# Draining a PSUM pair with two engines, one bank each, in a fused attention and maxout-FFN kernel

## The chip, the cores and the metric

The kernel runs on one core of one Trainium2 chip. The time is the device time of that core in microseconds; lower is better.

## The reference

Attention over 32 memory slots, for 8 batches of 8 heads, 576 positions and 64 dimensions, and behind it a feed-forward layer that takes the maximum of three products:

```python
def _attn_ref(q, k, v, phi):
    a = np.exp(phi - np.max(phi, axis=2, keepdims=True))
    a = a / (np.sum(a, axis=2, keepdims=True) + 1e-09)      # over the positions
    k_m = np.einsum('bhsm,bhsd->bhmd', a, k)
    v_m = np.einsum('bhsm,bhsd->bhmd', a, v)
    scores = (1.0 / np.sqrt(q.shape[-1])) * np.matmul(q, k_m.transpose(0, 1, 3, 2))
    attn = np.exp(scores - np.max(scores, axis=-1, keepdims=True))
    attn = attn / (np.sum(attn, axis=-1, keepdims=True) + 1e-09)
    return np.matmul(attn, v_m)
def _moe_ref(x, w1, w2, w3, w_out):
    h = np.maximum(np.maximum(x @ w1, x @ w2), x @ w3)
    return h @ w_out
```

`x` is the attention's output with the heads side by side: 4608 rows of 512 columns. `w1`, `w2`, `w3` are 512 x 768 and `w_out` is 768 x 512.

## The kernel before

The kernel never forms `x`. It multiplies the 32 value vectors of each head with the weights first (a *fold*), so that the feed-forward layer works on the attention weights: 256 numbers per position in place of 512. And it writes max(x w1, x w2, x w3) as x w3 + max(x (w1 - w3), x (w2 - w3), 0), so that only two products need a maximum and the third goes with `w_out` straight to the output.

Every step is a *piece*, named by a letter, a number and the batch, and the list of pieces at the end of the kernel is the order in which they are issued. Each engine runs its own instructions in this order and waits by semaphores for what it needs. There is no other scheduler. The pieces are:

- L, r: loads of phi, k, v and q on GpSimd's queue (`load_ph`, `load_kv`, `load_q`), and copies of k and v to a packed tile on GpSimd (`pack`). E: exponential of phi, on ScalarE.
- B, N, K: matmuls of phi's exponentials with k, v and ones (`att_kv`), the division on VectorE, and a transpose through TensorE with a small copy (`att_kv_t`, tile kvt).
- Q, S: transposes of q on VectorE, and the scores with their two exponentials on ScalarE (`att_score`, line 347). a, s, c, m, X: the softmax, that is a transpose, a sum and a reciprocal on VectorE, a product on GpSimd (line 414) and a transpose back into `attn` on VectorE (line 422), each for two groups of heads.
- D: folds (`fold`, line 445). D0 to D2 fold `w1 - w3` and `w2 - w3` in 512 columns each, D3 folds `w3 w_out`. A fold writes two banks of PSUM, one per group of heads.
- F: the first layer (`ffn1`, line 471), 12 pieces per batch of four matmuls with 288 columns, in two banks, one per half of the positions. Six are drained with relu into `h1`, and six by VectorE, which takes the maximum of the piece and `h1` (line 484).
- P, T: the second layer (`ffn2`, lines 502, 532, 541): 36 output tiles of 128 rows in one bank each, six matmuls with the hidden tile `hT` and two with `attn`. P starts a tile with three of them. T drains it and stores it from SyncE's queue.

PSUM has eight banks, and the digits behind `banks` give each piece its bank, or the first of two, in the order of the pieces. A piece whose bank is still being drained makes TensorE wait. The table `EVAC` says which engine drains which kind of piece, and `!` behind a piece swaps the two:

```python
EVAC = {"D": "avaaa", "T": "vavav", "K": "v", "W": "vvv", "O": "aaaa", "F": "aaaaaa"}
def evacuate(kind, n, swap, out_, in_, relu=False):
    if (EVAC[kind][n] == "a") != swap:
        ...   # ScalarE: activation with Relu, or copy
    ...       # VectorE: tensor_scalar_max, or tensor_copy
```

Of the kernel before, what the change touches and what calls it, by code (L numbers as in the profile page):

```python
# [15 lines left out]
def kernel(  # L16
# [12 lines left out]
    nc = tc.nc  # L29

    B, H, S, D = q.shape
    M = phi.shape[-1]
    P = 128
    NP = H // 2
    NG = NP // 2
    HP = P // 2
# [4 lines left out]
    FT = DF // P  # L41
    SH = S // 2
    BANK = 512
    HEAD = 3
# [96 lines left out]
    for i in range(P // M):  # L141
# [4 lines left out]
    banks = iter(  # L146
        "".join(
            """
            60606026024506010445024062406246024602434403424206026420462406240723043240604602
            46026402645260502624620640264024601642102461462624604624260462045260024062404206  # L150
            12640264014206502402605220462406420462036040432402677670
            """.split()
        )
    )
# [1 line left out]
    def one_bank():  # L156
        return psum[:, int(next(banks))]
# [13 lines left out]

    EVAC = {"D": "avaaa", "T": "vavav", "K": "v", "W": "vvv", "O": "aaaa", "F": "aaaaaa"}

    def evacuate(kind, n, swap, out_, in_, relu=False):

        if (EVAC[kind][n] == "a") != swap:
            if relu:
                nc.scalar.activation(out=out_, in_=in_, func=AF.Relu)  # L178
            else:
                nc.scalar.copy(out=out_, in_=in_)  # L180
        elif relu:
            nc.vector.tensor_scalar_max(out=out_, in0=in_, scalar1=0.0)  # L182
        else:
            nc.vector.tensor_copy(out=out_, in_=in_)  # L184

    def w3_t(f2, swap):
# [7 lines left out]
                )  # L194
        evacuate("W", f2, swap, w3T[:, 2 * f2 : 2 * f2 + 2], pt)

    def w3_o(j, swap):
        po = one_bank()
        for f in range(FT):
            nc.tensor.matmul(  # L200
                po,
                lhsT=w3T[:, f, j, :],
                rhs=wo_sb[:, f, :],
                start=(f == 0),
                stop=(f == FT - 1),
            )
        evacuate("O", j, swap, w3o[:, j, :], po)
# [115 lines left out]
    attns = {}  # L323
# [168 lines left out]

    heads = {}

    def ffn2_head(b, t):

        hT = hts[b // 2]
        c0 = (b % 2) * (S + HP) + t * P
        po = heads[b, t] = one_bank()
        for n in range(HEAD):  # L500
            fc = fts[b][n]
            nc.tensor.matmul(  # L502
                po,
                lhsT=hT[:, fc, c0 : c0 + P],
                rhs=wo_sb[:, fc, :],
                start=(n == 0),
                stop=False,
            )

    def ffn2(b, t, swap):  # L510


        hT, attn = hts[b // 2], attns[b // 2]
        c0 = S - HP if t == 4 else (b % 2) * (S + HP) + t * P
        if b == B - 1 and t == 3:
            return ffn2_last(b, c0)
        po = heads[b, t] if (b, t) in heads else one_bank()

        if t == 4:
            for g in range(NG):  # L520
                for u in range(2):
                    nc.tensor.matmul(  # L522
                        po[HP * u : HP * (u + 1)],
                        lhsT=attn[:, g, c0 + HP * u : c0 + HP * (u + 1)],
                        rhs=wp3s[b - 1 + u][:, g, :],
                        start=(g == 0),
                        stop=False,
                        tile_position=(0, HP * u),
                    )
        for n in range(HEAD if (b, t) in heads else 0, FT):  # L530
            fc = fts[b][n]
            nc.tensor.matmul(  # L532
                po,
                lhsT=hT[:, fc, c0 : c0 + P],
                rhs=wo_sb[:, fc, :],
                start=(n == 0 and t < 4),
                stop=(n == FT - 1 and t == 4),
            )
        if t < 4:
            for g in range(NG):  # L540
                nc.tensor.matmul(  # L541
                    po,
                    lhsT=attn[:, g, c0 : c0 + P],
                    rhs=wp3s[b][:, g, :],
                    start=False,
                    stop=(g == NG - 1),
                )
        ot = opool.tile([P, DM], FP32, name="ot")
        r0 = (b // 2) * 2 * S + c0
        rows = out[r0 : r0 + P, :]  # L550
        evacuate("T", t, swap, ot, po)
        nc.sync.dma_start(out=rows, in_=ot)
# [33 lines left out]
    def issue(b, n, swap):  # L586

        i = int(n[1:]) if len(n) > 1 else None
        {
            "I": lambda: [make_identity(nc, ident)]  # L590
            + [nc.gpsimd.memset(x[:, :, :, 2 * D : 2 * D + 1], 1.0) for x in kvrs],
            "Y": lambda: load_w(i) if i < 3 else load_wo(),
            "L": lambda: load_ph(b) if i == 0 else load_q(b) if i == 3 else load_kv(b, i - 1),
            "H": lambda: load_kv(b, i % 2, halves[i // 2]),
            "r": lambda: pack(b, i),
            "E": lambda: [att_exp(b, h) for h in (halves if b == 0 else [slice(0, NP)])],
            "B": lambda: att_kv(b, i),
            "N": lambda: att_kv_norm(b, i),
            "K": lambda: att_kv_t(b, swap, i),
            "Q": lambda: att_q(b, i),  # L600
            "S": lambda: att_score(b),
            "a": lambda: att_t(b, i),
            "s": lambda: att_sum(b, i),
            "c": lambda: att_rec(b, i),
            "m": lambda: att_mul(b, i),
            "X": lambda: (ones_mul if (b, i) in ONES else att_back)(b, i),
            "M": lambda: ones_sum(b, i),
            "R": lambda: ones_rec(b, i),
            "D": lambda: fold(b, i, swap),
            "F": lambda: ffn1(b, i, swap),  # L610
            "P": lambda: ffn2_head(b, i),
            "T": lambda: ffn2(b, i, swap),
            "W": lambda: w3_t(i, swap),
            "O": lambda: w3_o(i, swap),
            "V": lambda: w_diff(i),
            "G": lambda: wait_for(b, i),
            "Z": lambda: warm_up(i),
        }[n[0]]()


    for w in """
        E@0 H0@0 H2@0 L3@0 Z25@0 B0@0 I@0 N0@0 Z2@0 K0@0! Q0@0 Q1@0 Z9@0 S@0 Z2@0 M0@0 M1@0
        R0@0 Y2@0 G0@0 R1@0 W0@0 Y3@0 W1@0 W2@0 Z6@0 O1@0 H3@0 O3@0 O2@0 H1@0 X1@0 B1@0 X0@0
        N1@0 K1@0 O0@0 Y0@0 D1@0! D0@0! D3@0 F8@0 F10@0 F2@0 V0@0 F6@0 F0@0! Y1@0 D2@0 L0@1
        V2@0 L1@1 D4@0 V1@0 L3@1 F4@0 F3@0 L2@1 L1@2 F1@0 L2@2 F7@0 F5@0 F9@0 F11@0 P0@0 E@1
        B0@1 N0@1 T3@0 K0@1! Q0@1 Q1@1 L0@2 T0@0! S@1 L3@2 P1@0 V4@0 B1@1 a0@1 T1@0 s0@1 L3@3
        N1@1 c0@1 L2@3 a1@1 s1@1 K1@1 c1@1 m0@1 P2@0 X0@1 D1@1 D0@1 m1@1 D2@1 X1@1 T2@0! L1@3
        r0@2 F2@1! F10@1 F0@1! F4@1 F8@1 F5@1 r1@2 F6@1 L0@3 E@2 F9@1 F11@1 L0@4 L1@4 F1@1 F7@1
        P2@1 F3@1 B@2 N@2 D3@1 P3@1 P0@1 K@2! Q0@2 Q1@2 T0@1! S@2 a0@2 s0@2 c0@2 T4@1! m0@2
        a1@2 s1@2 c1@2 T2@1! D2@2 Q1@3 D0@2 D1@2! T3@1 m1@2 T1@1 X1@2 r1@3 L3@4 L2@4 X0@2 L2@5  # L630
        Q0@3 F4@2 F6@2 F0@2 F8@2 F7@2 r0@3 F1@2 F10@2 F5@2 E@3 F9@2 F11@2 F2@2 B@3 D3@2 N@3
        F3@2 L0@5 P3@2 K@3 P0@2 L1@5 S@3 T0@2 a0@3 r0@4 s0@3 c0@3 a1@3 s1@3 P2@2 m0@3 c1@3 D2@3
        m1@3 D1@3! L3@5 D0@3 T3@2! Q1@4 X0@3 X1@3 T2@2! Q0@4 T1@2 F10@3! r1@4 F2@3 F11@3 F6@3
        F8@3! F3@3 E@4 F4@3 F9@3 F5@3 F0@3 F7@3 B@4 D3@3 N@4 F1@3 P1@3 K@4 L1@6 L0@6 T1@3! r1@5
        E@5 S@4 D2@4 L2@6 a0@4 T4@3! r0@5 s0@4 L0@7 a1@4 P0@3 D1@4! B@5 s1@4 c1@4 D0@4 L1@7
        c0@4 Q1@5 m1@4 T0@3! N@5 Q0@5 K@5 P2@3 L2@7 X1@4 m0@4 S@5 X0@4 T2@3! F0@4 F2@4 a0@5
        F4@4! F6@4 r1@6 a1@5 P3@3 L3@6 D1@5! r0@6 D3@4 s1@5 D3@5! T3@3 F10@4 s0@5 c1@5 F3@4
        F8@4 c0@5 F11@4 F1@4 F7@4 F5@4 F9@4 m0@5 P1@4 P0@4 E@6 D0@5 m1@5 X0@5 B@6 D2@5 X1@5
        T0@4 T1@4 N@6 F6@5 F0@5 F7@5 F1@5 F4@5! Q0@6 F2@5 r0@7 F10@5 r1@7 T3@4! Q1@6 F5@5 F8@5!
        E@7 K@6! F9@5 T2@4! F3@5 S@6 F11@5 a1@6 B@7 L3@7 D2@6 N@7 a0@6 D0@6 T4@5! s0@6 K@7 Q1@7  # L640
        P0@5 s1@6 D1@7! D3@7 c1@6 c0@6 D0@7 Q0@7 m1@6 T0@5! m0@6 P1@5 S@7 T1@5 X1@6 a0@7 a1@7
        P3@5 X0@6 D2@7 D1@6! s0@7 c0@7 D3@6 s1@7 T3@5! m0@7 c1@7 F6@6 P2@5 m1@7 X0@7 X1@7 F10@6
        T2@5! F7@6 F10@7! F4@6 F0@7! F11@6 F8@6 F11@7 F0@6! F2@6 F5@6 F1@6 F3@6 F2@7! P3@6 F9@6
        P2@6 F1@7 F6@7 F7@7 T2@6 F4@7! T3@6! F8@7 T0@6! T1@6 F9@7 F5@7 F3@7 P0@7 T1@7! T0@7
        T2@7 T4@7! T3@7
    """.split():
        n, b = w.rstrip("!").split("@")
        issue(int(b), n, w.endswith("!"))


# [28 lines left out]
```

## Time and profile before

| what | value |
|---|---|
| median of 3 runs | 164.37 us (164.09 to 165.37) |
| the profiled execution | 163.68 us, of which the span is 161.9 |
| TensorE matmuls | busy 151.5 us (94%), 2056 records |
| VectorE | busy 106.4 us (66%), 203 instructions |
| ScalarE | busy 88.5 us (55%), 129 instructions |
| GpSimd | busy 69.6 us (43%) |
| granted TensorE clock | 1.0 |
| last matmul, then the last copy and store | 158.3 us, then 3.6 us |

The span runs from the first to the last instruction; the device time holds some 1.8 us more. A row of instructions gives the line of the kernel, engine, operation, tiles and shape, the count, the busy time and the mean of one in ns, and behind the bar the engine's idle time ahead of them with what ended it. Batch 0 takes up to about 38 us, with its loads and the preparation of the weights. From then on the batches overlap: while the softmax of one batch runs on ScalarE, VectorE and GpSimd, TensorE has output tiles and first-layer pieces of another.

### The profile page before, as it was taken

To read this page: it belongs to the slowest core of one execution; us is meant where nothing else is said; L and a number is where in the kernel's file an instruction comes from. 1 tells how busy PE (TensorE), PEld (TensorE's weight loads), DVE (VectorE), ACT (ScalarE), POOL (GpSimd) and SP (SyncE) were. 2 spreads that over 40 slices of the span, in tenths; PEclk is the share of its full clock that TensorE was granted. 3 is DMA by queue.
4 is the path that set the end of the run, shared out by engine and by line. 5 is a ranking of instruction groups with operands and counts; after the bars stand their busy time and mean duration, and the time that the engine had idled before them with its cause. 6 is when DMAs were issued, how large, how long until landed. Compare 5 with 4: busy or idle time off the path is not lost.

```text
span 161.9 us, 4816 instructions
## 1 busy us (share of the span) xinstructions
PE 151.5 (94%) x2056; PEld 85.6 (53%) x2080; DVE 106.4 (66%) x203; ACT 88.5 (55%) x129; POOL 69.6 (43%) x72
## 2 busy tenths in 40 slices
PE   7988799999899999999999999999999999999990
PEld 2443344664376436744774465656653467655450
DVE  2041704898969583959896959856897779863520
ACT  3206246926484769748567878477278963112010
POOL 7295213101879069746975914995004240000000
PEclk9999999999999999999999999999999999999999
DMA  5999999999999999999999999995911330024133
GB/s 152 176 203 201 203 211 214 276 208 208 260 312 236 208 244 382 282 212 215 314 278 208 292 287 306 235 208 140 188 72 65 130 112 21 0 84 158 74 143 132
DMA packets 21974, 31.77 MB, mean 196 GB/s; under 512 B 1216, under 2 KB 16576, under 8 KB 21952
## 3 DMA queue, kind: packets, MB, share of 16 engines
q0 software_dynamic: 16080, 21.43, 69.2%
q1 hardware_dynamic: 5728, 9.90, 17.4%
q8 instruction: 16, 0.26, 0.7%
q10 hardware_dynamic: 144, 0.13, 0.2%
q14 instruction: 6, 0.05, 0.1%
HBM read 39.32 MB, written 9.44 MB: 301 GB/s over the span
## 4 chain that ended last, share of the span: by engine, by line
PE 80%; DMA 10%; ACT 2%; issue 2%; DVE 2%; POOL 1%; ACTq 0%; POOLq 0%
PE psum L471 28%; PE psum L532 19%; PE psum L541 8%; PE psum L502 8%; DMA wo_sb<-in_moe_w_out_dram 7%; PE psum L445 6%; DMA kvo<-in_k_dram 4%; PE psum L254 4%; PE psum L200 3%; PE psum L338 2%; PE psum L522 1%; DVE sm L400 1%; PE psum L563 1%; ACT h L178 1%; PE psum L303 1%
## 5 line engine op out<-in xcount | busy, mean ns | idle before, releaser
L471 PE MATMUL psum<-attn,wp 128*128 128x288 bf16 x384 | 51.1, 286 | 0.1
L471 PEld LDWEIGHTS <-wp 128*128 128x128 bf16 x384 | 37.0, 98 | 14.1 <-issue 1.1
L484 DVE TENSOR_TENSOR hT<-psum,h 128x576 bf16<-128x576 f32 x48 | 34.2, 751 | 10.8 <-PE psum L471 9.8
L532 PE MATMUL psum<-wo_sb,hT 128*128 128x512 bf16 x131 | 34.1, 380 | 1.5 <-issue 1.4
L180 ACT CAST wp<-psum 128x1024 bf16<-128x1024 f32 (+1 forms) x30 | 28.2, 991 | 9.0 <-PE psum L445 7.2
L104 POOL COPY kvr<-kvo 128x2304 bf16<-128x2304 bf16 x12 | 25.3, 2112 | 10.5 <-PE psum L541 5.8
L178 ACT ACTIVATE h<-psum 128x576 bf16<-128x576 f32 x35 | 21.7, 661 | 14.3 <-PE psum L471 14.1
L180 ACT COPY ot<-psum 128x512 f32<-128x512 f32 x24 | 14.2, 596 | 22.8 <-PE psum L541 13.6
L414 POOL TENSOR_TENSOR t<-t,sm 128x576 bf16<-128x576 bf16 x14 | 16.1, 1155 | 22.7 <-DVE sm L409 22.4
L532 PEld LDWEIGHTS <-hT 128*128 128x128 bf16 x144 | 12.6, 98 | 16.7 <-issue 5.3
L541 PE MATMUL psum<-wp,attn 128*128 128x512 bf16 x62 | 18.4, 379 | 0.1
L502 PE MATMUL psum<-wo_sb,hT 128*128 128x512 bf16 x58 | 16.8, 379 | 0.5 <-issue 0.2
L167 PE MATMUL psum<-warm 128*128 128x512 bf16 x42 | 12.2, 447 | 1.4 <-DVE warm L136 1.2
L347 ACT ACTIVATE e<-psum 128x576 bf16<-128x576 f32 x16 | 9.6, 657 | 5.7 <-PE psum L338 5.7
L318 DVE STREAM_TRANSPOSE qT<-qq 128x576 f32<-128x576 f32 x16 | 11.8, 750 | 0.8 <-DMA qq<-in_q_dram 0.8
L182 DVE TENSOR_SCALAR h<-psum 128x576 bf16<-128x576 f32 x13 | 9.8, 752 | 3.2 <-PE psum L471 1.9
L111 POOL DMA_DIRECT2D qq<-in_q_dram x8 | 6.2, 774 | 12.8 <-DVE qT L318 7.6
L184 DVE COPY ot<-psum 128x512 f32<-128x512 f32 x11 | 7.5, 681 | 6.4 <-PE psum L541 4.4
L234 ACT ACTIVATE e<-ph 128x1152 bf16<-128x1152 f32 (+1 forms) x9 | 9.5, 1056 | 2.2 <-DMA ph<-in_phi_dram 2.2
L400 DVE TENSOR_REDUCE sm<-t 128x18 f32<-128x576 bf16 x14 | 10.4, 742 | 0.3
L541 PEld LDWEIGHTS <-attn 128*128 128x128 bf16 x62 | 6.1, 98 | 7.2
L98 POOL DMA_DIRECT2D kvo<-in_v_dram x9 | 6.7, 744 | 7.0 <-PE psum L254 4.0
(61 smaller groups left out, 135.5 us busy)
## 6 DMA issues: line engine op xcount, KB each, us to landing
out_dram<-ot SPq DMA_DIRECT2D x35, 256.0 KB, 5.4
qq<-in_q_dram POOLq DMA_DIRECT2D x8, 576.0 KB, 12.2
ph<-in_phi_dram POOLq DMA_DIRECT2D x7, 576.0 KB, 15.3
kvo<-in_k_dram POOLq DMA_DIRECT2D x7, 576.0 KB, 18.5
kvo<-in_v_dram POOLq DMA_DIRECT2D x7, 576.0 KB, 16.9
w_sb<-in_moe_w_dram POOLq DMA_DIRECT2D x3, 768.0 KB, 15.1
wo_sb<-in_moe_w_out_dram POOLq DMA_DIRECT2D x1, 768.0 KB, 10.7
ph<-in_phi_dram SPq DMA_DIRECT2D x2, 288.0 KB, 3.1
```

The costliest lines, as they stand in the source:

```text
L104: nc.gpsimd.tensor_copy(out=kvrs[b % 2][:, :, :, D * i : D * (i + 1)], in_=kvos[b % 2][:, 1 - i])
L167: nc.tensor.matmul(po[:, 0:BANK], lhsT=warm[:, 0:P], rhs=warm, start=True, stop=True)
L178: nc.scalar.activation(out=out_, in_=in_, func=AF.Relu)
L180: nc.scalar.copy(out=out_, in_=in_)
L318: nc.vector.transpose(out=s["qT"][:, j].rearrange("p j c r e -> p (j c r e)").bitcast(FP32), in_=loaded[b]["q"][:, j].rearrange("p j c d - ...
L400: nc.vector.tensor_reduce(out=sm, in_=s["t", g].rearrange("p n r e -> p n e r"), op=ALU.add, axis=mybir.AxisListType.X,)
L414: nc.gpsimd.tensor_tensor(out=t, in0=t, in1=s["sm", g].unsqueeze(2).to_broadcast([P, S // HP, R, 2]), op=ALU.mult,)
L471: nc.tensor.matmul(acc[:, h, 0:SH], lhsT=wps[b][:, g, w * DF + ft * P : w * DF + (ft + 1) * P], rhs=attn[:, g, c0 : c0 + SH], start=(g == ...
L484: nc.vector.tensor_tensor(out=hT[:, ft, (b % 2) * S : (b % 2 + 1) * S].rearrange("p (h n) -> p h n", h=2), in0=a, in1=s["h1", ft], op=ALU.max,
L502: nc.tensor.matmul(po, lhsT=hT[:, fc, c0 : c0 + P], rhs=wo_sb[:, fc, :], start=(n == 0), stop=False,)
L532: nc.tensor.matmul(po, lhsT=hT[:, fc, c0 : c0 + P], rhs=wo_sb[:, fc, :], start=(n == 0 and t < 4), stop=(n == FT - 1 and t == 4),)
L541: nc.tensor.matmul(po, lhsT=attn[:, g, c0 : c0 + P], rhs=wp3s[b][:, g, :], start=False, stop=(g == NG - 1),)
```

## The change

A new mark `^` behind a piece splits its drain: ScalarE takes one of its two banks and VectorE the other. `!` with `^` swaps the banks of a fold; behind an ffn1 piece it changes nothing. It stands behind 14 folds and 18 ffn1 pieces. The order of the pieces from batch 0's ffn1 on, and the banks, are new. `ffn2` is cut into parts (`ffn2_slots`, `ffn2_hidden`) that can be issued by themselves, and there is a `w3_o_head`; the new order uses neither `p` nor `J`, which would call them early. P still issues three matmuls, for 14 tiles in place of 22. Matmuls, loads and stores are the same ones. The program's instruction lists on GpSimd show the loads, packs and products in a new order, too.

```diff
     banks = iter(
         "".join(
             """
-            60606026024506010445024062406246024602434403424206026420462406240723043240604602
-            46026402645260502624620640264024601642102461462624604624260462045260024062404206
-            12640264014206502402605220462406420462036040432402677670
+            60606026024506010445024062406246024602434403626204204620620460246344632460440642
+            04602460245064602742064026042046405264624067026246024602462046364207406246026042
+            61620467246064035620420420460424206206246024601601010101
...
-    def evacuate(kind, n, swap, out_, in_, relu=False):
+    def evacuate(kind, n, how, out_, in_, relu=False):
+
+        swap = "!" in how
+        if "^" in how:
+            first = "" if EVAC[kind][n] == "a" else "!"
+            second = "!" if EVAC[kind][n] == "a" else ""
+            x = 1 if kind == "D" and swap else 0
+            evacuate(kind, n, first, out_[:, x], in_[:, x], relu)
+            evacuate(kind, n, second, out_[:, 1 - x], in_[:, 1 - x], relu)
+            return
 
         if (EVAC[kind][n] == "a") != swap:
...
-            "P": lambda: ffn2_head(b, i),
+            "P": lambda: ffn2_hidden(b, i, range(HEAD)),
+            "p": lambda: ffn2_slots(b, i),
+            "J": lambda: w3_o_head(i),
...
-        B0@1 N0@1 T3@0 K0@1! Q0@1 Q1@1 L0@2 T0@0! S@1 L3@2 P1@0 V4@0 B1@1 a0@1 T1@0 s0@1 L3@3
-        N1@1 c0@1 L2@3 a1@1 s1@1 K1@1 c1@1 m0@1 P2@0 X0@1 D1@1 D0@1 m1@1 D2@1 X1@1 T2@0! L1@3
-        r0@2 F2@1! F10@1 F0@1! F4@1 F8@1 F5@1 r1@2 F6@1 L0@3 E@2 F9@1 F11@1 L0@4 L1@4 F1@1 F7@1
...
+        L1@2 N0@1 L2@2 Q1@1 Q0@1 V4@0 K0@1! T0@0! S@1 P1@0 a0@1 s0@1 B1@1 a1@1 N1@1 L0@2 c0@1
+        T1@0 s1@1 L3@2 K1@1 m0@1 P2@0 c1@1 m1@1 D0@1 D1@1^ X0@1 X1@1 r0@2 D2@1 T2@0! L3@3 F2@1^
+        F4@1 F3@1 F6@1^ F10@1 F0@1!^ F11@1 L1@3 F7@1 r1@2 F8@1 F9@1 L2@3 F5@1 F1@1 P0@1 E@2 B@2
+        D3@1^ L0@3 T4@1! L2@4 N@2 Q0@2 Q1@2 K@2! T0@1 S@2 a0@2 s0@2 P3@1 Q0@3 a1@2 L3@4 P2@1
+        c0@2 L0@4 D1@2! s1@2 m0@2 c1@2 m1@2 D0@2!^ D2@2^ X0@2 X1@2 T3@1! T1@1 r0@3 T2@1 F0@2
...
+        F5@2 F3@2 K@3! L1@5 P0@2 S@3 L0@5 a0@3 a1@3 s0@3 c0@3 s1@3 c1@3 m0@3 m1@3 T1@2 D0@3!^
+        X0@3 r1@4 D2@3 r0@4 D1@3! T0@2 E@4 X1@3 Q1@4 T3@2! L3@5 F8@3!^ L0@6 F4@3^ F6@3 r1@5
...
+        F9@5 F5@5 F11@5 E@7 T2@4! r1@7 D3@6!^ Q0@7 B@7 S@6 N@7 T3@4 K@7! P3@5 a1@6 Q1@7 D2@6^
+        a0@6 s1@6 s0@6 S@7 a0@7 c0@6 T3@5 D0@7! m0@6 D0@6!^ D2@7 s0@7 c1@6 a1@7 T4@5! X0@6 P1@5
+        m1@6 X1@6 D1@6! D3@7^ D1@7^ T1@5! c0@7 T2@5! m0@7 F0@6^ F2@6^ s1@7 X0@7 F4@6 c1@7
...
+        F3@7 F8@7 F8@6 F1@7 F6@7^ F9@7 F9@6 F5@7 F11@7 T0@6 T3@6 F7@7 T2@6 T1@6 T2@7! T0@7 T1@7
+        T4@7 T3@7
     """.split():
-        n, b = w.rstrip("!").split("@")
-        issue(int(b), n, w.endswith("!"))
+        n, b = w.rstrip("!^").split("@")
+        issue(int(b), n, w[len(n) + 1 + len(b) :])
```

More of the change, by code (lines that the diff above doesn't have):

```diff
@@ L195, in w3_t, with w3_o_head @@
         evacuate("W", f2, swap, w3T[:, 2 * f2 : 2 * f2 + 2], pt)
+    w3_heads = {}
+    def w3_o_head(j):
+        po = one_bank()
+        for f in range(HEAD):
+            nc.tensor.matmul(
+                po,
+                lhsT=w3T[:, f, j, :],
+                rhs=wo_sb[:, f, :],
+                start=(f == 0),
+                stop=False,
+            )
+        w3_heads[j] = po, HEAD
     def w3_o(j, swap):
-        po = one_bank()
-        for f in range(FT):
+        po, done = w3_heads.pop(j, (None, 0))
+        po = one_bank() if po is None else po
+        for f in range(done, FT):
             nc.tensor.matmul(
@@ L493, with tile_parts, ffn2_slots @@
     heads = {}
[L495 to L513, printed above, removed]
-        c0 = S - HP if t == 4 else (b % 2) * (S + HP) + t * P
[L515 to L520, printed above, removed]
+    def tile_parts(b, t):
+        c0 = S - HP if t == 4 else (b % 2) * (S + HP) + t * P
+        po, done = heads.get((b, t)) or (one_bank(), set())
+        heads[b, t] = po, done
+        return po, done, c0
+    def ffn2_slots(b, t, last=False):
+        po, done, c0 = tile_parts(b, t)
+        attn = attns[b // 2]
+        for g in range(NG):
+            if t == 4:
                 for u in range(2):
@@ L529, in ffn2, with ffn2_hidden @@
                     )
-        for n in range(HEAD if (b, t) in heads else 0, FT):
+            else:
+                nc.tensor.matmul(
+                    po,
+                    lhsT=attn[:, g, c0 : c0 + P],
+                    rhs=wp3s[b][:, g, :],
+                    start=(g == 0 and not done),
+                    stop=(last and g == NG - 1),
+                )
+        done.add("slots")
+    def ffn2_hidden(b, t, ns, last=False):
+        po, done, c0 = tile_parts(b, t)
+        hT = hts[b // 2]
+        for n in ns:
             fc = fts[b][n]
@@ L535, in ffn2 @@
                 rhs=wo_sb[:, fc, :],
-                start=(n == 0 and t < 4),
-                stop=(n == FT - 1 and t == 4),
-            )
[L539 to L547, printed above, removed]
+                start=(n == ns[0] and not done),
+                stop=(last and n == ns[-1]),
+            )
+        done.update(ns)
+    def ffn2(b, t, swap):
+        if b == B - 1 and t == 3:
+            return ffn2_last(b, S + HP + t * P)
+        po, done, c0 = tile_parts(b, t)
+        if t == 4 and "slots" not in done:
+            ffn2_slots(b, t)
+        first = "slots" in done
+        left = [n for n in range(FT) if n not in done]
+        ffn2_hidden(b, t, left, last=first)
+        if not first:
+            ffn2_slots(b, t, last=True)
         ot = opool.tile([P, DM], FP32, name="ot")
@@ L623 @@
         R0@0 Y2@0 G0@0 R1@0 W0@0 Y3@0 W1@0 W2@0 Z6@0 O1@0 H3@0 O3@0 O2@0 H1@0 X1@0 B1@0 X0@0
-        N1@0 K1@0 O0@0 Y0@0 D1@0! D0@0! D3@0 F8@0 F10@0 F2@0 V0@0 F6@0 F0@0! Y1@0 D2@0 L0@1
-        V2@0 L1@1 D4@0 V1@0 L3@1 F4@0 F3@0 L2@1 L1@2 F1@0 L2@2 F7@0 F5@0 F9@0 F11@0 P0@0 E@1
-        B0@1 N0@1 T3@0 K0@1! Q0@1 Q1@1 L0@2 T0@0! S@1 L3@2 P1@0 V4@0 B1@1 a0@1 T1@0 s0@1 L3@3
-        N1@1 c0@1 L2@3 a1@1 s1@1 K1@1 c1@1 m0@1 P2@0 X0@1 D1@1 D0@1 m1@1 D2@1 X1@1 T2@0! L1@3
-        r0@2 F2@1! F10@1 F0@1! F4@1 F8@1 F5@1 r1@2 F6@1 L0@3 E@2 F9@1 F11@1 L0@4 L1@4 F1@1 F7@1
@@ L629 @@
[L629 to L645, printed above, removed]
+        N1@0 K1@0 O0@0 Y0@0 D1@0! D0@0! D3@0 F8@0 F10@0 F2@0 V0@0 F6@0 F0@0! Y1@0 L0@1 D2@0
@@ new lines @@
+        L1@1 V2@0 D4@0 F4@0 V1@0 F3@0 F1@0 F11@0 F5@0 E@1 F9@0 F7@0 P0@0 B0@1 L3@1 T3@0 L2@1
+        L1@2 N0@1 L2@2 Q1@1 Q0@1 V4@0 K0@1! T0@0! S@1 P1@0 a0@1 s0@1 B1@1 a1@1 N1@1 L0@2 c0@1
[3 more added lines that the diff above has]
+        c0@2 L0@4 D1@2! s1@2 m0@2 c1@2 m1@2 D0@2!^ D2@2^ X0@2 X1@2 T3@1! T1@1 r0@3 T2@1 F0@2
@@ new lines @@
+        F10@2 Q1@3 F1@2 F8@2 F9@2 F6@2 F4@2! r1@3 E@3 F11@2 F7@2 F2@2 B@3 N@3 D3@2 L1@4 L2@5
+        F5@2 F3@2 K@3! L1@5 P0@2 S@3 L0@5 a0@3 a1@3 s0@3 c0@3 s1@3 c1@3 m0@3 m1@3 T1@2 D0@3!^
+        X0@3 r1@4 D2@3 r0@4 D1@3! T0@2 E@4 X1@3 Q1@4 T3@2! L3@5 F8@3!^ L0@6 F4@3^ F6@3 r1@5
+        F9@3 L1@6 F5@3 F2@3 F0@3 F10@3 F7@3 F1@3 Q0@4 P2@2 B@4 N@4 D3@3^ r0@5 F3@3 T2@2! K@4!
+        F11@3 P0@3 S@4 T0@3! L2@6 L1@7 a1@4 a0@4 L3@6 s1@4 s0@4 E@5 c0@4 L0@7 c1@4 T1@3 D0@4^
+        m0@4 m1@4 B@5 N@5 r0@6 D2@4 Q0@5 D3@4 T4@3! K@5 r1@6 X0@4 P2@3 Q1@5 D2@5^ X1@4 D1@4!
@@ new lines @@
+        T2@3 S@5 F6@4!^ F0@4 F8@4 F7@4 F9@4 F4@4!^ F10@4 F11@4 F5@4 P3@3 a0@5 E@6 s0@5 F2@4
+        F3@4 F1@4 L2@7 c0@5 T3@3 a1@5 s1@5 m0@5 c1@5 T1@4 D3@5^ X0@5 m1@5 B@6 D0@5 D1@5! N@6
+        L3@7 X1@5 Q0@6 T0@4! Q1@6 F2@5^ F3@5 F8@5 F0@5!^ F6@5^ K@6! F10@5 F1@5 F7@5 r0@7 F4@5^
+        F9@5 F5@5 F11@5 E@7 T2@4! r1@7 D3@6!^ Q0@7 B@7 S@6 N@7 T3@4 K@7! P3@5 a1@6 Q1@7 D2@6^
+        a0@6 s1@6 s0@6 S@7 a0@7 c0@6 T3@5 D0@7! m0@6 D0@6!^ D2@7 s0@7 c1@6 a1@7 T4@5! X0@6 P1@5
+        m1@6 X1@6 D1@6! D3@7^ D1@7^ T1@5! c0@7 T2@5! m0@7 F0@6^ F2@6^ s1@7 X0@7 F4@6 c1@7
@@ L646 @@
+        F10@6!^ F6@6 F5@6 F11@6 m1@7 P0@5 X1@7 F7@6 F1@6 T0@5! F3@6 F0@7^ F10@7^ F4@7 F2@7^
+        F3@7 F8@7 F8@6 F1@7 F6@7^ F9@7 F9@6 F5@7 F11@7 T0@6 T3@6 F7@7 T2@6 T1@6 T2@7! T0@7 T1@7
+        T4@7 T3@7
     """.split():
-        n, b = w.rstrip("!").split("@")
-        issue(int(b), n, w.endswith("!"))
+        n, b = w.rstrip("!^").split("@")
+        issue(int(b), n, w[len(n) + 1 + len(b) :])
 _INS = ['q', 'k', 'v', 'phi', 'moe_w1', 'moe_w2', 'moe_w3', 'moe_w_out']
```

## The prediction

> **What bounds the kernel now.** I read the page first: the busy shares and the slices.
>
> ```profile
> PE 151.5 (94%) x2056; PEld 85.6 (53%) x2080; DVE 106.4 (66%) x203; ACT 88.5 (55%) x129; POOL 69.6 (43%) x72
> DVE  2041704898969583959896959856897779863520
> DMA  5999999999999999999999999995911330024133
> ```
>
> TensorE is busy 94% of the span, and the chain that ended last lies on it for 80%. VectorE's mean of 66% hides slices of 8 and 9 in the middle. The DMA engines are full for the first two thirds: loads land one behind the other, about 3 us each. Then the busy time by batch, cut where the scores (S) of batches 1 to 7 start: window, TensorE, weight loads, VectorE, ScalarE, GpSimd, clock, DMA.
>
> ```profile
> 38.64:54.95 16.31, 15.58 (x287) 9.32 (x290) 13.80 (x26) 9.83 (x14) 10.97 (x10) 1.00 1.17 254
> 54.95:70.30 15.35, 15.14 (x220) 8.86 (x221) 10.40 (x21) 12.13 (x18) 10.19 (x9) 1.00 1.14 284
> 70.30:86.60 16.30, 16.09 (x234) 9.15 (x234) 13.04 (x26) 10.73 (x14) 11.49 (x9) 1.00 1.17 254
> 86.60:93.20 6.60, 6.28 (x151) 2.93 (x153) 5.93 (x15) 5.20 (x7) 6.09 (x6) 1.00 1.17 260
> 93.20:117.10 23.90, 23.58 (x287) 14.69 (x291) 18.21 (x32) 14.89 (x22) 12.59 (x9) 1.00 1.03 230
> 117.10:124.60 7.50, 7.34 (x172) 3.39 (x172) 6.61 (x15) 5.92 (x9) 0.97 (x1) 1.00 0.20 75
> ```
>
> In these 86.0 us TensorE is idle for 1.95 us by the records, and much of that isn't idle time: line 532 has 131 matmul records for 144 weight loads, and a gap of 0.16 us stands wherever one is missing. VectorE is busy 68.0 of the 86.0 us (79%), ScalarE 58.7. So TensorE sets the pace at full clock with next to no gaps, and a change that leaves its matmuls alone can win only those gaps. Where real ones are, the chain of waits shows: start, length, what.
>
> ```profile
> 38.64 0.54 PE psum L338 x20
> 39.18 0.65 ACT e L347
> ...
> 40.36 0.75 DVE sm L400
> ...
> 42.61 0.14 DVE kvt L184
> ...
> 42.80 0.84 PE psum L445 x24
> ...
> 62.18 5.40 PE psum L471 x44
> ```
>
> At 39 to 43 us the end hangs on ScalarE and VectorE (softmax of batch 1, then the transposed k and v), and TensorE waits a little. In the last line 44 ffn1 matmuls take 0.123 us each, so a piece (four) takes 0.49.
>
> **What the change costs.** These rows give the drains (shapes, count, busy, mean ns):
>
> ```profile
> L484 DVE TENSOR_TENSOR hT<-psum,h 128x576 bf16<-128x576 f32 x48 | 34.2, 751 | 10.8 <-PE psum L471 9.8 <-ACT h L178 0.5
> L180 ACT CAST wp<-psum 128x1024 bf16<-128x1024 f32 x28 | 27.1, 1020 | 9.0 <-PE psum L445 7.2 <-DVE rden L274 1.8
> L178 ACT ACTIVATE h<-psum 128x576 bf16<-128x576 f32 x35 | 21.7, 661 | 14.3 <-PE psum L471 14.1
> L182 DVE TENSOR_SCALAR h<-psum 128x576 bf16<-128x576 f32 x13 | 9.8, 752 | 3.2 <-PE psum L471 1.9 <-ACT h L178 0.7 <-ACT wp L180 0.6
> L184 DVE COPY ot<-psum 128x512 f32<-128x512 f32 x11 | 7.5, 681 | 6.4 <-PE psum L541 4.4 <-ACT e L347 1.9
> L184 DVE CAST wp<-psum 128x1024 bf16<-128x1024 f32 x3 | 3.7, 1225 | 1.9 <-PE psum L445 1.9
> L180 ACT CAST wp<-psum 128x512 bf16<-128x512 f32 x2 | 1.2, 588 | 0.0
> L580 DVE COPY ot<-psum 128x256 f32<-128x256 f32 x1 | 0.4, 425 | 2.1 <-PE psum L571 2.1
> L583 ACT COPY ot<-psum 128x256 f32<-128x256 f32 x1 | 0.4, 372 | 1.2 <-PE psum L571 1.2
> ```
>
> *Prices of a half.* A fold's half is 512 columns: 0.59 on ScalarE and 0.68 on VectorE. An ffn1 half is 288 columns, which no row shows; between 256 (0.37 and 0.43) and 576 (0.66 and 0.75) the straight line gives 0.40 and 0.46. Bounds are those rows.
>
> *The count.* The order lists name 14 folds and 18 ffn1 pieces with the mark for both engines. Of the 33 folds, 30 were on ScalarE and 3 on VectorE; now 17, 2 and 14 on both. Of the 48 ffn1 pieces with relu it was 35 and 13; now 28, 2 and 18 on both. Three more of the small kvt copies go to ScalarE. VectorE: 18 x 0.46 + 14 x 0.68 - 11 x 0.75 - 1.23 - 3 x 0.35 = +7.3 us. ScalarE: 18 x 0.40 + 14 x 0.59 - 7 x 0.66 - 13 x 1.02 + 3 x 0.48 = -1.0 us. So ScalarE gets no freer to speak of and VectorE pays. Back to back, VectorE's instructions overlap a little (five maxima of 0.75 in 3.56 us, 0.71 each), so its durations count at some 0.91. Summed along the order lists from S@1 to S@7, the matmul work is 83.3 before and 78.9 after, VectorE's durations 74.4 and 79.1. At 0.91 the 74.4 give the 68.0 of the windows; after, 72.3 us stand against about 81 us of TensorE: 89% in place of 79%. What hides the 7.3 us is VectorE's idle time there, which falls from 18 to 9 us, about 1.5 per batch; nearly 1 of that is its wait for the exponentials after each S (1.3 us from S to the first transpose), so little cover is left.
>
> The Trainium skill, Perfetto Trace Analysis, Optimizing Scalar/DVE Operations, speaks on both sides: larger operations if the engine is saturated, broken up ones if it isn't but causes bubbles elsewhere. It puts the overhead of an instruction on PSUM at about 125 ns for VectorE; the rows for 256 and 512 columns give 169 (2 x 425 - 681). By the page the 32 halves would cost VectorE 32 x 0.044 = 1.4 us less. The rows decide, and here both of its conditions are near.
>
> *What halving gains.* A bank pair comes back two ffn1 pieces later in the tightest places: 0.98 us. A whole drain is 0.66 on ScalarE or 0.75 on VectorE, plus 0.1 to 0.2 to hand over; halved it is 0.46 plus the same. That matters only where the drain starts late. TensorE's own work from S@1 to its last matmul at 158.3, at the best paces of the chain (84 pieces x 0.49 = 41.2, 34 output tiles at 1.73 or 1.86 = 59.3, 28 folds x 0.27 = 7.6, the small rest 9.1) is 117.2 us of 119.7. So 2.5 us is the bound of the gain and 0 the other; part is the 0.6 us wait for kvt at 42.8, which stays (its chain has the same instructions). I take -0.6, near the low end, as the rows show TensorE back to back.
>
> *What the new order costs.* I follow three places, S at 0. Batch 1: kvt at +4.2 as before; folds D0, D1 0.27 each, hand over 0.2, then VectorE's half of D1 (0.68) stands ahead of both transposes back (0.42 each): attn is done at +6.5, while TensorE gets to the first ffn1 piece at +6.2, where the old order had the first transpose ahead of the folds. 0.3 late. Batch 3: first transpose +1.3, six softmax pieces 2.9 (56.27 to 59.17 in batch 2 of before), D0's half 0.63, one transpose 0.42, output tile 0 of batch 2 0.65, the other transpose: +6.25. TensorE's pieces in between now sum to 5.8 (0.42 + 1.73 + 0.8 + 1.08 + 1.73), where they were 6.9; the piece's second pair of matmuls needs the late half 0.25 later, so 0.2 to 0.3 late. Batches 6 and 7 share one stretch: from the first transpose VectorE has 10.4 us queued up to the output tile whose bank F4@6 takes, at S@6 +12.7; TensorE gets there at +12.7. No margin; 0.3. Batches 2 and 4 come out 0.1 late each, batch 5 has 13 us and nothing. Sum +1.1; bounds 0 and 2.5 (each place late by twice that, as whatever is late on VectorE stands ahead of the next maxima).
>
> *What moves besides.* The loads on GpSimd's queue go out in another order (q of batch 3 behind the first pack, k of batch 4 behind v of batch 4, both packs before the next loads). At 3.06 us per load from the 31.4 us where phi of batch 1 landed, phi of batch 5 lands near 86.5 (83.0 before) and its exponential is needed at about 89; k of batch 4 near 77.5 (71.3), its pack done at 79.6 and needed at 81. Hidden with 1 to 2 us to spare; -0 to +1. Fewer output tiles are started early (14 in place of 22): same matmuls, 0. The last tile's second half now takes the bank that the tile before it frees, 0.1 at most. Switches between matmul shapes: 57 in place of 58, 0. Output stores: the same number from SyncE.
>
> **Sum.** -0.6 + 1.1 = +0.5 us on the profiled execution of 163.68 (161.9 span and 1.8 around it): 164.2. The median shown is 164.37, 0.69 above that execution, so 164.9.
>
> **Rivals.** (1) Slower by over 1%: VectorE's queue. At 89% with waits for the exponentials, a late half holds the maxima behind it, those hold banks, and TensorE stops in every batch. It decides once VectorE's idle time from S@1 to S@7 is used up, that is if halves and hand-overs cost some 0.25 us more each than the rows (32 x 0.25 = 8). For: VectorE's work equals 92% of TensorE's (72.3 of 78.9). Against: such chains ran to 0.1 us in before (batch 3: attn done at +7.2, first ffn1 at +7.1). Price: 2.5 and no gain: 166.9. (2) Faster by over 1%: nearly all of TensorE's 2.5 us comes back and the order costs 0.3: -2.2, 162.2. For: banks come back 0.2 to 0.4 sooner at 32 places. Against: half of the 2.5 is records and the kvt wait. (3) The halves don't run together, as one engine's queue is behind when the other's is free: banks come back no sooner, no gain: +1.1, 165.5. (4) A load lands late: 2 us at phi of batch 5 blocks ScalarE's queue at the exponential, less the 1 us to spare: +1, and with the rest 165.9.
>
> **Chances.** Forecast 0.53, (1) 0.24, (2) 0.07, (3) 0.10, (4) 0.06. A measurement of this kernel tells about 1% from no change. Within 1% (162.7 to 166.0) are the forecast, (3) and half of (4), 0.66; slower (1) and the rest, 0.27; faster 0.07. The range from 162.9 to 167.2 leaves out (2) and the far part of (1).
>
> **What would show it.** TensorE's work from S@1 stays at 117 us. VectorE's busy time is 111 to 114, ScalarE's 86 to 89. Halves last 0.40, 0.46, 0.59 and 0.68. Waits of the ffn1 matmuls for VectorE's transposes appear in batches 1 and 3. I am wrong if VectorE stays at 106, if TensorE's gaps go away (2) or if they grow in every batch (1).

## The result, and the profile after

The changed kernel takes 164.75 us (median of 22 runs, 164.21 to 165.62) against 164.36 (22 runs of before, 163.83 to 165.37). The ratio is 1.0028, with a 95% interval of 1.0015 to 1.0042: about 0.46 us slower, clear of noise and well within 1%. The forecast was 164.9. Its total was right; two of the terms that made it were not, and that they cancel is luck.

The page's busy line and slices after, as they were shown of before:

```profile
PE 154.1 (95%) x2080; PEld 85.8 (53%) x2080; DVE 110.3 (68%) x220; ACT 87.5 (54%) x144; POOL 69.5 (43%) x72
DVE  2041704798868789879795887997889897853120
DMA  5999999999999999999999999999031231013333
```

VectorE has 3.9 us more, and most of its slices of 3, 5 and 6 in the middle have become 7 and 8. This execution has a record for every matmul (2080). The groups of the new halves (shapes, count, busy, mean ns):

```profile
L193 DVE CAST wp<-psum 128x512 bf16<-128x512 f32 x14 | 9.2, 667 | 2.4 <-PE psum L469 2.3
L191 DVE TENSOR_SCALAR h<-psum 128x288 bf16<-128x288 f32 x18 | 7.9, 446 | 1.8 <-PE psum L495 1.7
L189 ACT CAST wp<-psum 128x512 bf16<-128x512 f32 x14 | 8.0, 591 | 4.0 <-PE psum L469 3.9
L187 ACT ACTIVATE h<-psum 128x288 bf16<-128x288 f32 x18 | 7.4, 417 | 1.8 <-PE psum L495 1.6
```

The prices were 0.68, 0.46, 0.59 and 0.40. Then the windows between the starts of the scores of batches 1 to 7 and the last matmul (TensorE, weight loads, VectorE, ScalarE, GpSimd, clock, DMA):

```profile
39.01:56.54 17.53, 17.11 (x311) 9.44 (x316) 13.54 (x28) 10.54 (x18) 10.69 (x10) 1.00 1.17 251
56.54:70.89 14.35, 14.35 (x230) 8.44 (x237) 13.33 (x26) 9.45 (x14) 10.29 (x10) 1.00 1.15 274
70.89:86.36 15.47, 15.47 (x235) 8.92 (x241) 13.18 (x27) 9.91 (x16) 12.24 (x9) 1.00 1.16 264
86.36:95.75 9.39, 9.35 (x194) 4.15 (x200) 7.12 (x18) 7.72 (x11) 5.73 (x7) 1.00 1.15 275
95.75:117.66 21.91, 21.91 (x355) 14.56 (x360) 18.33 (x36) 14.69 (x26) 12.24 (x8) 1.00 0.94 205
117.66:121.06 3.40, 3.40 (x71) 1.48 (x77) 2.77 (x8) 2.26 (x5) 0.00 (x0) 1.00 0.23 82
121.06:159.13 38.07, 38.05 (x297) 21.18 (x297) 24.41 (x45) 15.43 (x28) 4.61 (x4) 1.00 0.25 93
```

Behind the first window TensorE is busy for 102.53 of 102.59 us: no gap is left to speak of. All that it waits for after the start of batch 1 stands in the first window, and the chain of waits shows the place (start, length, what):

```profile
51.67 0.73 PE psum L278 x69
52.41 0.27 PE psum L469 x8
52.67 0.58 ACT wp L189
53.30 0.59 PE psum L533 x3
53.89 1.40 PE psum L557 x6
```

Line 278 is B of batch 2, line 469 the fold D3 of batch 1, line 533 the first matmuls of the shared output tile T4. T4 reads `wp3`, which D3 writes, and the new order issues it right behind D3: TensorE stands until ScalarE's half (0.58 us) is done. T4 takes 2.57 us there and 1.86 in the other batches, so the wait costs 0.7. In the old order five pieces of TensorE lay between the two (P3, P0 and T0 of batch 1, K and S of batch 2).

From the start of the scores of batch 1 to the last matmul it is 119.6 us before and 120.1 after. What lies ahead of it differs from one execution to the next, whatever the order: the first score matmul of batch 1 starts at 38.6 to 40.9 us in the five profiles of the old order (39.4 on average) and at 39.0 to 40.5 in the eight of the new one (39.5). Experiments are therefore compared over this stretch, besides by their times.

### The profile page after: what moved, and what is told of

It is laid out like the page before. It is cut to its first block, busy times and chain, and to the rows that moved or that the text cites. A ratio compares the mean times of both kernels' runs of the same rounds, so it can differ in the third digit from the quotient of the medians.

```text
span 162.8 us, 4888 instructions
## 1 busy us (share of the span) xinstructions
PE 154.1 (95%) x2080; PEld 85.8 (53%) x2080; DVE 110.3 (68%) x220; ACT 87.5 (54%) x144; POOL 69.5 (43%) x72
## 4 chain that ended last, share of the span: by engine, by line
PE 77%; DMA 15%; POOL 2%; DVE 1%; ACT 1%; issue 1%; POOLq 0%
PE psum L557 28%; PE psum L495 28%; DMA w_sb<-in_moe_w_dram 12%; PE psum L542 8%; PE psum L469 5%; DMA kvo<-in_k_dram 4%; PE psum L278 3%; PE psum L362 2%; POOL kvo L98 1%; PE psum L533 1%; PE psum L593 1%; PE psum L327 1%; DVE t L416 1%; POOL wo_sb L124 0%; DVE sm L424 0%
## 5 line engine op out<-in xcount | busy, mean ns | idle before, releaser
L557 PE MATMUL psum<-wo_sb,hT 128*128 128x512 bf16 x210 | 53.2, 380 | 0.0
L495 PE MATMUL psum<-attn,wp 128*128 128x288 bf16 x384 | 49.9, 286 | 0.1
L495 PEld LDWEIGHTS <-wp 128*128 128x128 bf16 x384 | 37.0, 98 | 12.5 <-issue 1.1
L557 PEld LDWEIGHTS <-hT 128*128 128x128 bf16 x210 | 18.9, 98 | 22.4 <-issue 5.4
L187 ACT ACTIVATE h<-psum 128x576 bf16<-128x576 f32 (+1 forms) x46 | 23.9, 563 | 7.8 <-PE psum L495 7.0
L189 ACT CAST wp<-psum 128x512 bf16<-128x512 f32 (+1 forms) x31 | 23.3, 798 | 6.8 <-PE psum L469 6.6
L193 DVE CAST wp<-psum 128x512 bf16<-128x512 f32 (+1 forms) x16 | 11.5, 733 | 4.3 <-PE psum L469 4.2
L191 DVE TENSOR_SCALAR h<-psum 128x288 bf16<-128x288 f32 (+1 forms) x20 | 9.4, 478 | 2.5 <-PE psum L495 1.7
```

The lines of the kernel that those rows point to most:

```text
L495: nc.tensor.matmul(acc[:, h, 0:SH], lhsT=wps[b][:, g, w * DF + ft * P : w * DF + (ft + 1) * P], rhs=attn[:, g, c0 : c0 + SH], start=(g == ...
L557: nc.tensor.matmul(po, lhsT=hT[:, fc, c0 : c0 + P], rhs=wo_sb[:, fc, :], start=(n == ns[0] and not done), stop=(last and n == ns[-1]),)
```

## The experiments

Each ratio compares with runs of the kernel before that were taken beside that experiment. A difference to the changed kernel is the difference of the two ratios, times 164.4 us.

**1. The fold ahead of B.** Only this pair is swapped:

```diff
- ... P0@1 E@2 B@2 D3@1^ L0@3 T4@1! ...
+ ... P0@1 E@2 D3@1^ B@2 L0@3 T4@1! ...
```

> The new order, but with the fold D3 of batch 1 issued ahead of the matmuls B of batch 2 instead of behind them, so that the shared output tile T4 of batch 1 no longer follows the fold whose result it reads. Theory A (the whole loss of the new order is TensorE's wait of 0.7 us for this fold's drain at 52.6 us; everything else came out even): the wait goes, B's 0.7 us of matmuls cover the drain, and the time falls by 0.5 to 0.7 us below the changed kernel, to about 0.1 to 0.3 us below the kernel before (ratio 0.998 to 0.9995). Rival B (VectorE's longer queue costs the time, as the prediction summed it, and the wait only shows it there): the wait moves to the next piece, the ratio stays at 1.002 to 1.004.

Measured: ratio to before 1.0008 (0.9993 to 1.0022), 164.29 us. Its chain of waits at the same place:

```profile
52.26 0.41 PE psum L467 x8
52.67 0.67 PE psum L276 x70
53.34 0.62 PE psum L531 x4
```

T4 (line 531 here) follows B without a gap. From the scores of batch 1 to the last matmul it takes 119.6 us, which is the 119.6 of before. The ratio falls between the ranges of the two theories, and its interval overlaps that of the changed kernel (1.0028), so the times alone don't decide. The trace does, for theory A: the 0.5 us that the stretch had grown by are gone with this one wait. Of the further gain over before that A forecast nothing is seen.

**2. All drains whole, in the new order.** The 32 marks are taken out (`w.replace("^", "")`). The whole drains go where the table and `!` send them: 8 of the 14 folds to ScalarE and 6 to VectorE, 12 of the 18 ffn1 pieces to ScalarE and 6 to VectorE.

> The new order and banks with every split drain whole again (the 32 marks are taken out; each piece goes to the engine that the table and the ! name). Theory A (the order was built on the early return of the banks, and there the split is worth something): late drains stop TensorE at several places, for one the tile T4 of batch 1 waits 0.4 us longer (1.02 for 0.59); 0.8 to 2.5 us slower than the changed kernel, ratio to before 1.008 to 1.018. Rival C (the halves gain nothing, as banks wait for the later of two queues anyway): within 0.4 us of the changed kernel, ratio 1.000 to 1.005. The forecast's own term for the halves was 0.6 us.

Measured: 1.0298 (1.0268 to 1.0327), 168.80 us. That is 4.4 us slower than the changed kernel, more than either theory said. The wait at T4 grew, from 0.58 us of ScalarE's drain to 1.02:

```profile
53.62 1.02 ACT wp L187
54.69 0.59 PE psum L531 x3
```

So in the order made for them the halves are worth 4.4 us against whole drains on these engines; another choice of engines for the whole drains was not tried. The forecast's term of 0.6 compared them with the old order, and meant something else.

**3. The halves in the old order.** The new `evacuate` and the mark behind the same 32 pieces, with the order and banks of before.

> The order and banks of before, with the split drain at the same 32 pieces as in the changed kernel. VectorE gets some 4 to 7 us more work and the order is not made for it. Theory A (TensorE sets the pace, and VectorE's idle time in each batch covers the halves): within 0.4 us of before, ratio 0.998 to 1.003, with VectorE's busy time at 110 to 112. Rival B (VectorE's queue is what costs): a late half holds the transposes and maxima behind it, 1 us or more, ratio 1.006 or more.

Measured: 1.0420 (1.0395 to 1.0446), 171.01 us, 6.8 us slower than before: rival B, far above its least. VectorE was busy for 112.9 us, and TensorE's waits for VectorE between the scores of batch 1 and the end sum to 4.4 us, where before has 0.3. The timeline of VectorE shows one place (start, length, line, operation; in brackets the idle time ahead of it):

```profile
93.25 0.27 DVE L416 RECIPROCAL sm<-sm 128x18 f32<-128x18 f32 x1
94.22 0.69 DVE L191 CAST wp<-psum 128x512 bf16<-128x512 f32 x1 [0.70 <-PE psum L452]
94.82 0.26 DVE L416 RECIPROCAL sm<-sm 128x18 f32<-128x18 f32 x1
94.99 0.72 DVE L325 STREAM_TRANSPOSE qT<-qq 128x576 f32<-128x576 f32 x1
95.64 0.13 DVE L281 RECIPROCAL rden<-psum 128x2 f32<-128x2 f32 x1
95.80 0.29 DVE L285 TENSOR_TENSOR kvn<-psum,rden 128x128 bf16<-128x128 f32 x1
```

VectorE runs its pieces in order. It reaches a fold's half before TensorE has made the fold, stands for 0.70 us, and then needs 0.69 for it. The softmax of batch 4 and the division (`kvn`) of batch 5, for which TensorE waits, stand behind it. In the kernel before, ScalarE drains the whole fold and VectorE goes on:

```profile
90.30 0.39 DVE L409 RECIPROCAL sm<-sm 128x18 f32<-128x18 f32 x2
90.60 0.72 DVE L318 STREAM_TRANSPOSE qT<-qq 128x576 f32<-128x576 f32 x1
91.25 0.13 DVE L274 RECIPROCAL rden<-psum 128x2 f32<-128x2 f32 x1
91.41 0.29 DVE L278 TENSOR_TENSOR kvn<-psum,rden 128x128 bf16<-128x128 f32 x1
```

There the division `kvn` starts 4.9 us behind the first score matmul of batch 4 (86.56), in kernel 3 6.3 us behind it (89.52): 1.4 us later, one half of it the wait and the other the drain.

**4. Every ffn1 half twice on VectorE.** `if kind == "F": evacuate(kind, n, second, ...)` once more.

> The changed kernel with each of VectorE's 18 ffn1 halves done twice (the second writes the same numbers again), 18 x 0.45 = 8.1 us more on VectorE, 15 of them from batch 1 on to batch 6. It measures how much cover VectorE still has. Theory A (cover of about 14 us between S of batch 1 and S of batch 7, by the windows): most is hidden, 0 to 2 us, ratio to before 1.003 to 1.014. Rival B (hardly any cover left): most of it shows, 4 to 8 us, ratio 1.027 to 1.05.

Measured: 1.0264 (1.0241 to 1.0286), 168.39 us. VectorE's busy time rose by 7.4 us (110.3 to 117.7) and the time by 3.9 over the changed kernel: about half of the added work shows. Both theories missed, B by less. So the 14 us in which VectorE is idle in the windows are no full cover. TensorE's waits on the doubled halves (0.7 us) and on the maxima (0.5 us) account for 1.2 of the 3.9 us; the rest stands in no wait that the trace names.

**5. VectorE out of the way.** The transposes, sums, reciprocals and products of the second softmax are left out; `attn` is a copy of the exponentials. The fold is ahead of B.

> The fold D3 of batch 1 ahead of B of batch 2 as in e1, and the division of the second softmax left out from batch 1 on: the transposes, sums, reciprocals and products are gone and one copy on VectorE puts the exponentials where the attention weights go. TensorE's instructions and their order stay; VectorE loses about 20 us and the chain from the scores to the first layer shrinks from 5 to under 1 us. It shows what TensorE would take with VectorE out of the way, read in the trace from the start of the scores of batch 1 to the last matmul (119.6 us before and in e1). Theory A (order and halves are at TensorE's own pace, what is left over the 117.2 us that its pieces sum to is the switching between shapes): 118.8 to 119.6 us. Rival D (short waits hidden inside the back-to-back matmuls still add up to 1 us or more, which a better order could win): 117.3 to 118.5 us.

One profiled execution. Two lines of windows, from the scores of batch 2 to the last matmul, first of this kernel and then of the changed one:

```profile
57.14:159.55 102.41, 101.13 (x1285) 58.69 (x1301) 64.11 (x120) 59.42 (x98) 31.46 (x25) 1.00 0.74 184
56.54:159.13 102.59, 102.53 (x1301) 58.74 (x1301) 79.14 (x156) 59.47 (x98) 45.11 (x37) 1.00 0.74 184
```

With 15 us less on VectorE in this stretch TensorE takes 102.4 us instead of 102.6. In batch 1 the copy itself came late (TensorE waited 0.9 us for it), so over the whole stretch, for which both theories had named their ranges, it is 120.2 and meets neither. Behind batch 1 the reading is that of theory A: the changed kernel is at TensorE's own pace, and its pieces there sum to about 101.3 at the paces of the prediction. The 1.1 to 1.3 us above the sum are no waiting for VectorE's softmax. The drains stayed as they were in this run; that TensorE doesn't wait for them either is read from the window of the changed kernel alone (busy for 102.53 of 102.59 us).

**6 and 7. Which halves.** The marks are taken out at the 14 folds (6), or at the 18 ffn1 pieces (7). As in 2, the whole folds go 8 to ScalarE and 6 to VectorE, the whole ffn1 pieces 12 and 6.

> The changed kernel with the 14 split folds whole again, the 18 ffn1 pieces still split. With all 32 whole the time rose by 4.4 us. If the folds' halves are what the order leans on (a whole fold takes 1.02 on ScalarE or 1.2 on VectorE, and output tiles and scores take its banks soon after): 2.5 to 4 us slower than the changed kernel, ratio to before 1.018 to 1.028. If the ffn1 halves are (banks come back after two pieces): 0 to 1.5 us slower, ratio 1.003 to 1.012.

> The changed kernel with the 18 split ffn1 pieces whole again, on ScalarE, and the 14 folds still split. VectorE loses 18 x 0.45 = 8 us, ScalarE's drains grow from 0.42 to 0.66. If the folds' halves carry the gain: 0 to 1.5 us slower than the changed kernel, ratio 1.003 to 1.012. If the ffn1 halves do: 2.5 to 4 us slower, ratio 1.018 to 1.028. If VectorE's load were what costs (rival B), it would be faster than the changed kernel.

Measured: folds whole 1.0221 (1.0168 to 1.0274), 3.2 us over the changed kernel; ffn1 whole 1.0083 (1.0052 to 1.0114), 0.9 us over it. The folds' halves carry most of it. The expectation for 7 had all 18 pieces on ScalarE; with 6 of them whole on VectorE, its busy time fell by 2.6 us (110.3 to 107.7) and not by 8, so 7 says little on VectorE's load. In the chain of kernel 6 TensorE waits behind one whole fold after the other on ScalarE:

```profile
91.90 0.59 ACT ot L187
92.48 0.92 ACT wp L187
93.41 0.04 issue
93.45 0.62 PE psum L531 x4
...
97.65 1.03 ACT wp L187
```

Its largest waits after the start of batch 1 are for whole folds on either engine (us in total, times, longest), and those of kernel 2 are the same:

```profile
PE psum L555 <- DVE wp L191: 1.3, 2, 1.0
PE psum L531 <- ACT wp L187: 0.9, 2, 0.8
```

**8. Three places mended.** Besides the fold, `N1@1` stands ahead of `a1@1`, `K1@1` is `K1@1!`, and the last tile's second half takes bank 6 in place of 1.

> The changed kernel with three places mended: the fold D3 of batch 1 ahead of B of batch 2 (as in e1), the division N of batch 1's v on VectorE ahead of the second transpose and its kvt copy on ScalarE, and the last output tile's second half in a bank that is free. By the trace of the changed kernel the three are worth 0.5, 0.2 and 0.1 us. Theory A (only such single places are left to win): 0.7 to 0.9 us below the changed kernel, ratio to before 0.997 to 0.9995. Rival B (VectorE's queue costs): no more than e1, 1.0005 or above.

Measured: 0.9992 (0.9964 to 1.0019), 164.53 us: no difference to before that can be told, and so no kernel shown to beat both. The ratio lies in theory A's range, but the trace doesn't bear A out. From the scores of batch 1 to the last matmul it is 119.7 us, as in 1. The first ffn1 matmul of batch 1 starts 5.9 us behind the scores in place of 6.0, but the scores of batch 2 start 17.07 us behind those of batch 1 in both 1 and 8: what the earlier start won was lost again ahead of D3, which in both waits for VectorE to drain the ffn1 piece before it in the same banks. The free bank at the end did save 0.1 (2.03 to 1.91 us for the last tile).

**9. The kernel before, once more.**

> The kernel before, unchanged, profiled once more. The profiles so far differ most ahead of batch 1: its scores start at 38.6 us in the one profile of before and at 39.0 to 40.5 us in those of the other kernels, whose pieces up to there are nearly the same. If this is chance of the loads of the weights: somewhere from 38.6 to 40.5 us here, too. From there to the last matmul 119.6 us, as in the first profile.

The first matmuls of the scores of batch 1 started at 39.0 us, but their chain goes through the load of q, which landed at 38.1, and the rest followed at 39.6:

```profile
15.52 22.59 DMA qq<-in_q_dram
38.10 0.02 issue
38.13 1.45 DVE qT L318 x2
39.58 0.04 issue
39.62 0.42 PE psum L338 x14
```

From 39.6 it is 119.6 us to the last matmul again. So the kernel before, too, starts batch 1 0.4 to 1 us later in one execution than in another.

**10 and 11. Which halves in the old order.** Kernel 3 with the marks at the 18 ffn1 pieces alone, or at the 14 folds alone.

> The order and banks of before with the split drain at the 18 ffn1 pieces alone. All 32 splits in this order cost 6.8 us. If they cost by VectorE's work alone (about 4 of 7 us of it are the ffn1 halves, as 11 pieces were on VectorE whole): 3 to 4 us slower than before, ratio 1.018 to 1.026. If they cost by where the fold's half stands in VectorE's queue (ahead of the divisions of the next batch, waiting for its matmuls): under 1.5 us, ratio 1.000 to 1.009.

> The order and banks of before with the split drain at the 14 folds alone. If by VectorE's work alone: 3 to 4 us slower than before, ratio 1.018 to 1.026. If by the place in the queue (the trace with all 32 shows VectorE waiting 0.3 and 0.7 us for fold matmuls at 86.4 and 94.2 us, with the divisions of batches 4 and 5, the kvt copies and the scores behind it): 4.5 to 6.5 us slower, ratio 1.027 to 1.040.

Measured: 1.0089 (1.0058 to 1.0121), 1.5 us, for ffn1; 1.0358 (1.0310 to 1.0407), 5.9 us, for the folds. VectorE got 0.6 us more busy time by the one and 5.7 by the other, and not 4 and 3 as expected, so by work alone the folds could cost more, too, and the two ratios don't separate the theories. Where the time goes does. Between the first score matmuls of batches 3 and 4, 4 and 5, and 6 and 7, kernel 11 takes 1.4, 1.4 and 1.7 us longer than before, which is 4.5 of the 5.3 us by which the stretch grew. Kernel 3 takes the same 1.4, 1.4 and 1.7 us longer there, and kernel 10 at most 0.2 in each. So the folds' halves cost at a few places and not evenly with the work; the second of them is the place shown under 3, where VectorE waits 0.70 us in 3 and 0.68 in 11.

## Why the prediction was right, and where it was not

*What bounds the kernel.* Right. TensorE sets the pace, and taking 15 us off VectorE changed 0.2 us behind batch 1 (5).

*Prices and count.* The prices were right: 0.42, 0.45, 0.59 and 0.67 for the halves. ScalarE came out at 87.5 as said. VectorE's 110.3 is just below the 111 to 114. Its durations rose by 6.3 us (115.5 to 121.8 over the whole execution, for +7.3 forecast), of which 4.0 came out as busy time, as its instructions overlapped more: the busy time is 0.91 of the durations, where before it is 0.92.

Between the starts of the scores of batches 1 and 7 VectorE was busy 83% and not 89%, with 13.8 us idle and not 9. The 79.1 of the prediction was the wrong sum for that: it follows the order list, and in the trace 2.5 us of what the list has ahead of S@7 (the half of D2, a transpose and two sums) run behind its start. By time the durations there are 75.7 us, with 68.3 busy. So rival 1's cover was larger than the prediction thought.

The 1.4 us worked out beside these prices compares unlike things; no term of the sum used it. The Trainium skill, Perfetto Trace Analysis, Optimizing Scalar/DVE Operations, gives its 125 ns as an engine-busy time and puts profiled latency at about twice that. The 169 ns come from profiled durations, and the halves measured here give 162 (446 and 667 ns for 288 and 512 columns), between the two.

*Gain of the halves, -0.6.* Wrong: against before there was none. The step read the 2.5 us over TensorE's summed pieces as waiting that could be won. Behind batch 1 it is not waiting for VectorE (5), and before has about 1.2 there as well (103.1 us from the scores of batch 2, with pieces that sum to 101.9). What halving does is allow an order that is 4.4 us slower with whole drains (2), and that order had nothing left to win.

*Cost of the order, +1.1.* Wrong in its places. This is VectorE in batch 1 after the change:

```profile
42.75 0.21 DVE L193 COPY kvt<-psum 128x128 bf16<-128x128 bf16 x1
42.87 0.26 DVE L433 RECIPROCAL sm<-sm 128x18 f32<-128x18 f32 x1
43.74 0.69 DVE L193 CAST wp<-psum 128x512 bf16<-128x512 f32 x1 [0.60 <-PE psum L469]
44.35 0.83 DVE L446 STREAM_TRANSPOSE attn<-t 128x288 f32<-128x288 f32 x2
```

The half does stand ahead of both transposes, as foreseen, and VectorE waits 0.6 us for it. But attn is done at 45.2, 6.2 us behind the scores and not 6.5, and the first ffn1 matmul starts at 45.0, without a wait. In batch 3 the transposes end at +6.0 (76.9 us) and not +6.25, with the ffn1 piece at +5.9. In the stretch of batches 6 and 7 VectorE is done with the output tile at +12.5 (130.1 us) and not +12.7, ahead of F4, and TensorE has no gap. So each walk put VectorE 0.2 to 0.3 late. In batch 1 about 0.15 of it is kvt, which was ready for TensorE at +4.0 (43.0 us) and not at +4.2 as before; the walks also took durations one after the other that overlap in the rows by 0.05 to 0.1 us each. All of the 1.1 went. In its place comes the 0.7 at T4, which the walks missed. They followed the chain from the scores to the first layer and the return of banks, and never asked for each piece moved closer to another whether it reads what that one writes.

*The sum.* +0.5 was forecast and about +0.46 measured. That they agree is luck, as the errors cancelled: the sum that the traces show is 0 for gain and chains, and +0.7 at T4 less 0.15 at the start of batch 1's ffn1 (6.03 us behind the scores in place of 6.18).

*Rivals.* (1), VectorE's queue, did not happen in the changed kernel, but its mechanism is real: the same halves in an order not made for them cost 6.8 us, most of it in waits for VectorE (3), and doubling some costs 3.9 (4). That puts the changed kernel close to the edge that the rival named. (2) was not to be had, since the larger part of the 2.5 us was no gap. (3), halves that don't run together, did happen in part. In 7 of the 14 folds and 7 of the 18 ffn1 pieces of the changed kernel the second half starts after the first has ended. For D3 of batch 3 VectorE had the division of batch 4 ahead of its half:

```profile
83.41 0.58 ACT L189 CAST wp<-psum 128x512 bf16<-128x512 f32 x1 [1.76 <-PE psum L469]
84.31 0.68 DVE L193 CAST wp<-psum 128x512 bf16<-128x512 f32 x1
```

Both banks are back 1.6 us after the drain began, where a whole drain takes 1.02. The rival's price was the 1.1 of the new order without a gain, and that cost turned out to be nothing. Since the 32 marks are still worth 4.4 us (2), they can't rest on both halves running at the same time everywhere. Which of the 32 carry it was not tried one by one. (4), a late load: the start of batch 1 moved by 1 us and more with kernels of either order; after it TensorE waited for no load in the changed kernel.

## What to carry to other kernels

A half drained by a second engine can shorten the return of a bank, but it also stands in that engine's queue and waits there for its matmul: the same 32 halves were worth 4.4 us in one order and cost 6.8 in another, so the split and the order are one change. When a list of pieces is moved, go through every pair that came closer together and ask first for the data that one hands the other, then for banks and queues. And before counting the gaps of the bounding engine as winnable, take the other engine's work away once and see whether they close. A total that fits says little about its terms: look for each of them in the trace.

## What the runs showed that was not expected

The profile of before has 2056 of 2080 matmul records and that of the changed kernel all of them, so TensorE's busy time (151.5 and 154.1 us) and its gaps can't be compared between the two; the distance from the first scores to the last matmul can. That start itself moved between 38.6 and 40.9 us over the profiled executions, which is more than the change. In two profiles of the same kernel the chain ahead of it went through different loads, of k and `w_out` the first time, and of the other weights and q in 9.
